# All of the second batch's keys transposed on TensorE and scored in float32

## The chip, the cores and the metric

The kernel runs on one core of a Trainium2 chip. The metric is the device time of one execution in microseconds (us); below it is compared by the median of several runs. The engines have short names in the profile: PE is TensorE (its weight loads are PEld), DVE is VectorE, ACT is ScalarE, POOL is GpSimd, SP is SyncE, which issues nearly all DMAs here.

## The reference

Two stages follow each other for 4 batches of 11456 tokens of width 128. First an attention through 49 agents: the agents attend to the keys and gather values, then the queries attend to the agents. Then a mixture of 8 experts of width 1024, of which each token takes one.

```python
def sm(a, b):
    s = scale * (a @ b.transpose(0, 2, 1))
    s = s - s.max(-1, keepdims=True)
    e = np.exp(s)
    return e / (e.sum(-1, keepdims=True) + 1e-09)
a2k = sm(agents, k)
agent_v = a2k @ v
q2a = sm(q, agents)
x = q2a @ agent_v
...
logits = xn @ en.T / tau
expert_idx = np.argmax(logits, axis=1)
...
h = np.maximum(x[mask] @ w1[e], 0.0)
out[mask] = gate_w[mask, None] * (h @ w2[e])
```

## The kernel before, in words

**Units.** The tokens of a batch are cut into `NU` = 12 units: 11 of 128 x 8 tokens and a last one of 96 x 2. A unit of keys, values or queries is one load of 512 KB by SP into one of `LB` = 10 buffers of a ring, which all three kinds share. `room()` lets a new load into the program's order when the unit that held the buffer has been marked by `used()` some steps earlier.

**Keys.** The scores of keys against agents need the keys with the width of 128 on the partitions, so each unit is transposed first. There are two ways to do it, and `by_pairs(b, u)` chooses for each unit of batches 1 to 3.

- `k1_f32`: PE transposes the 8 blocks of the unit as float32 into PSUM (`pe_T`, L420, tile `fTp`), ACT copies them to SBUF in two pieces (L427, tile `fT`), PE multiplies them with the agents in float32 (`scores`, L438; 16 matmuls of 64 columns of weights), ACT copies the scores out (L460), and DVE updates a running maximum (L410). The unit's buffer is marked as used as soon as the transposes are in the program.
- `k1_pairs`: ACT squares the unit to find a scale (L526), three small DVE instructions make a power of two of it (L251 to L255), ACT writes the scaled unit as float16 (L530), DVE writes the float16 remainder (L536), both into the tile `ks`, of which there are `XS` = 2. SP issues a DMA that transposes it in SBUF (L541, tile `kT`). PE multiplies with three float16 matmuls for each block (L550 to L552), ACT copies the scores out with a scale (L556), DVE updates the maximum (L410). The buffer is marked as used only after L536.

**The rest of a batch's preparation.** When all key units have a maximum, `k_max` reduces it; `k2_unit` takes exponentials and multiplies them with the values (L572, L577, L586); `av_chain` and `pick_expert` make one expert's weights ready for the batch in the form the main loop wants (tiles `gh`, `gl`, `w2p`, `vm`; loads of `w1s` and `w2s`, L907 and L908; rank and selection on DVE and ACT, L807, L809, L819, L895).

**The main loop.** A batch has 23 tiles of 512 tokens. A tile has two steps; each is a pair of matmuls (L1218, L1219, tile `hp`), an activation on ACT (L1222), a remainder on DVE (L1223), and 12 small matmuls into the output tile `yp` (L1246 to L1248). I call such a step an hp, and count the program's order of each engine in hp: 46 to a batch. Around it stand the queries (`q_unit`: transposes L420, scores L438, exponentials on ACT and a cast L955, remainder on POOL L956, a DMA transpose of `tt` by SP, L967), a proof that no token was treated wrongly (L1089 on PE, L1093 on ACT or L1095 on DVE), and the stores of the result (L1268).

**Order.** Batch b + 1 is prepared while batch b runs through the main loop. `plan()` gives each unit a due time in steps of the loop; `loader()` asks for loads 18 steps ahead of that if the ring has room. Batch 1's first `NEXT` = 4 key units are done before the main loop, all in float32. A scheduler then orders each engine's instructions when the kernel is built, and each engine runs its list strictly in that order. So a wait of one instruction holds up all that stand behind it on its engine.

`by_pairs` is the whole rule before:

```python
def by_pairs(b, u):
    return u % 2 == 0
...
spawn((k1_pairs if by_pairs(b, u) else k1_f32)(b, u))
```

Of the kernel before, what the change touches and what calls it, by code (L numbers as in the profile page):

```python
# [29 lines left out]
def kernel(ctx: ExitStack, tc: tile.TileContext, q, k, v, agents, emb, tau, w1, w2, out):  # L30
# [1559 lines left out]
        return sorted(kv), qs  # L1590

    def by_pairs(b, u):
        return u % 2 == 0

    AHEAD2 = 18

# [16 lines left out]
    def keys():  # L1613

        start = now[0] // 2
        for at, kind, b, u in plan()[0]:
            while now[0] // 2 < start + at:
                yield 1
            if kind == "k":
                if not hasattr(batches[b], "blks"):  # L1620
                    k_start(b)
                spawn((k1_pairs if by_pairs(b, u) else k1_f32)(b, u))
            else:
                kb = batches[b].blks[0]
                if u == 0:
                    while kb.k1 < NU:
                        yield 1
                    yield from k_max(b, pss, 1)
                    yield 1
                spawn(k2_unit(b, u, pool, (3, 4)))  # L1630
                if u == NU - 1:
                    spawn(after_keys(b))
# [31 lines left out]
    with nullcontext():  # L1664
        due = []
        for i in range(len(ticks) + LAG):
            if i < len(ticks):
                b, t, r = ticks[i]
# [12 lines left out]
            while due and due[0][0] <= i:  # L1681
                _, b, t, f = due.pop(0)
# [44 lines left out]
```

## Time and profile before

| | us |
|---|---|
| median of 3 runs | 694.39 |
| the runs | 689.1, 694.39, 697.4 |
| the profiled execution | 692.29 |
| its span, first to last instruction | 690.5 |

The profiled execution took 1.8 us more than its span, and lies 2.1 us below the median. The stages in it: batch 0's keys, values and weights up to about 87 us, then the main loops of the four batches, of which batch 0's lasts to about 245 us. Batch 1's and the first of batch 2's keys are worked on in this stretch. A row of the windows view has, for each engine, its busy time in the stretch and the number of instructions, then the granted clock of PE and the busy share of the DMA engines.

### The profile page before, as it was taken

What the parts mean: (1) busy time and instruction counts of PE and PEld (TensorE: products, weight loads), DVE (VectorE), ACT (ScalarE), POOL (GpSimd) and SP (SyncE); (2) the same over time, 40 slices, a digit from 0 to 9 for tenths busy, and PEclk for the clock granted to TensorE, in tenths of its full rate; (3) what the DMA queues carried; (4) which work ended last, traced back from release to release, by engine and by line L of the source; (5) the groups of instructions that cost most, each with busy time, mean ns of one, the idle gap of its engine ahead of it and who ended that gap; (6) DMA issues with size and microseconds to landing.
All of it is one profiled execution on the core that took longest, in us unless ns stands there. A gap on an engine that the chain in (4) does not pass through costs nothing. (4 is left out here: it accounts for less than half of the span.)

```text
span 690.5 us, 23309 instructions
## 1 busy us (share of the span) xinstructions
PE 644.2 (93%) x9168; PEld 529.4 (77%) x9168; DVE 535.2 (78%) x1492; ACT 488.8 (71%) x1350; POOL 322.0 (47%) x565
## 2 busy tenths in 40 slices
PE   8999898999898799999999889999999989998996
PEld 6887786877787588778888768787888768786785
DVE  4755996875577998856677999897567899878993
ACT  3455677887678946878778965778656973878941
POOL 6000146575402654666533452667473452977400
PEclk9998999999999999999999999999999999999999
DMA  8988279859478459986896529959576246134221
GB/s 337 298 270 299 70 151 251 232 145 265 112 255 227 102 159 248 229 206 140 244 310 197 138 84 224 219 133 249 149 217 212 83 120 156 43 83 139 77 81 71
DMA packets 163137, 124.74 MB, mean 181 GB/s; under 512 B 82874, under 2 KB 139280, under 8 KB 163026
## 3 DMA queue, kind: packets, MB, share of 16 engines
q1 hardware_dynamic: 162706, 123.01, 65.5%
q8 instruction: 73, 1.20, 0.7%
q14 instruction: 38, 0.31, 0.1%
q0 software_dynamic: 320, 0.23, 0.1%
HBM read 80.26 MB, written 23.79 MB: 151 GB/s over the span
## 5 line engine op out<-in xcount | busy, mean ns | idle before, releaser
L1223 DVE SCALAR_TENSOR_TENSOR hl<-hp,hh 128x512 f16<-128x512 f32 (+1 forms) x184 | 122.9, 669 | 30.2 <-ACT hh L1222 29.4
L1246 PE MATMUL yp<-w2p,hh 128*128 128x128 f16 x720 | 138.8, 221 | 1.8 <-ACT hh L1222 1.7
L1247 PE MATMUL yp<-w2p,hh 128*128 128x128 f16 x720 | 138.4, 221 | 0.0
L1093 ACT ACTIVATE under<-vp 128x320 f16<-128x320 f32 (+1 forms) x268 | 118.4, 442 | 26.9 <-PE vp L1089 24.2
L1248 PE MATMUL yp<-w2p,hl 128*128 128x128 f16 x720 | 136.2, 221 | 0.3 <-DVE hl L1223 0.3
L1222 ACT ACTIVATE hh<-hp 128x512 f16<-128x512 f32 (+1 forms) x184 | 107.6, 589 | 39.6 <-PE hp L1219 29.8
L1089 PE MATMUL vp<-vm,tt 128*128 128x320 f16 x360 | 96.1, 301 | 9.3 <-DVE vmin L1095 3.2
L438 PEld LDWEIGHTS sp<-aT_all,fT 128*64 128x64 f32 x2336 | 81.6, 140 | 20.7 <-issue 10.1
L438 PE MATMUL sp<-aT_all,fT 128*64 128x49 f32 x2336 | 94.7, 227 | 1.7 <-DVE rt L998 0.4
L427 ACT COPY fT<-fTp 128x512 f32<-128x512 f32 (+1 forms) x136 | 74.8, 573 | 27.6 <-PE fTp L420 19.7
L1246 PEld LDWEIGHTS <-hh 128*128 128x128 f16 x720 | 71.8, 100 | 18.4 <-ACT hh L1222 6.9
L1248 PEld LDWEIGHTS <-hl 128*128 128x128 f16 x720 | 71.7, 100 | 12.2 <-issue 2.9
L1247 PEld LDWEIGHTS <-hh 128*128 128x128 f16 x720 | 71.6, 99 | 5.2 <-issue 0.3
L1218 PE MATMUL hp<-tt,gh 128*128 128x512 f16 (+1 forms) x184 | 69.1, 376 | 4.1 <-ACT under L1093 2.1
L956 POOL TENSOR_TENSOR e<-qe,e 128x392 f16<-128x392 f32 (+1 forms) x46 | 40.2, 873 | 69.3 <-ACT e L955 66.5
L1040 POOL TENSOR_TENSOR nrm<-qq,half 128x16 f32<-128x16 f32 (+2 forms) x28 | 69.3, 2475 | 0.2
L1219 PE MATMUL hp<-tt,gl 128*128 128x512 f16 (+1 forms) x184 | 69.0, 376 | 0.0
L1261 DVE TENSOR_TENSOR ot<-yp,gs 128x512 f32<-128x512 f32 (+1 forms) x92 | 61.6, 671 | 7.2 <-PE yp L1248 4.3
L1237 PE MATMUL yp<-lin,tt 128*128 128x128 f16 x720 | 61.6, 220 | 2.2 <-DVE ot L1261 2.2
L1001 POOL TENSOR_TENSOR rt<-rt 128x384 f32<-128x384 f32 (+1 forms) x48 | 40.7, 848 | 45.5 <-DVE rt L998 43.2
L420 PE MATMUL fTp<-ident,qt 128*128 128x128 f32 (+1 forms) x344 | 53.3, 278 | 7.0 <-ACT under L1093 4.0
L1093 ACT ACTIVATION_READ_ACCUMULATOR under<-vp 128x1 f32 (+1 forms) x268 | 55.0, 205 | 0.0
(354 smaller groups left out, 1538.6 us busy)
## 6 DMA issues: line engine op xcount, KB each, us to landing
kt<-in_k_dram SPq DMA_DIRECT2D x44, 512.0 KB, 6.3
vt<-in_v_dram SPq DMA_DIRECT2D x44, 512.0 KB, 6.2
out_dram<-ot SPq DMA_DIRECT2D x88, 256.0 KB, 3.7
qt<-in_q_dram SPq DMA_DIRECT2D x42, 512.0 KB, 5.3
w1s<-in_moe_w_dram SPq DMA_DIRECT2D x9, 512.0 KB, 3.6
w2s<-in_moe_w_dram SPq DMA_DIRECT2D x9, 512.0 KB, 4.9
q<-in_q_dram SPq DMA_DIRECT2D x2, 512.0 KB, 11.9
tt<-e SPq DMA_TRANSPOSE x46, 3.3
```

The source lines that it names most:

```text
L427: act.copy(dst, tp[:, : m * p])
L438: i = pe.matmul(out=s[h : h + w, c * A : (c + 1) * A], lhsT=xT[:, c * p + h : c * p + h + w], rhs=rhs, start=True, stop=True, skip_group_c ...
L1040: pool.tensor_tensor(out=nrm, in0=quad, in1=half[:, :n], op=ALU.pow)
L1089: pe.matmul(out=z[:p, :FV], lhsT=tts[b, u][:, c * p : (c + 1) * p], rhs=bt.vm, start=True, stop=True)
L1093: act.activation(under[:p], z[:p, :FV], AF.Relu, scale=-1.0, accum_out=bt.vsum[:p, at])
L1218: pe.matmul(out=hp[:, :m], lhsT=bt.gh[:, fs], rhs=tt, start=True, stop=False)
L1219: pe.matmul(out=hp[:, :m], lhsT=bt.gl[:, fs], rhs=tt, start=False, stop=True)
L1222: h_last[:] = [act.activation(hh[:, :m], hp[:, :m], AF.Relu)]
L1223: dve.scalar_tensor_tensor(out=hl[:, :m], in0=hp[:, :m], scalar=0.0, in1=hh[:, :m], op0=ALU.max, op1=ALU.subtract)
L1246: pe.matmul(out=y, lhsT=hh[:, cs], rhs=wh, start=False, stop=False, skip_group_check=True)
L1247: pe.matmul(out=y, lhsT=hh[:, cs], rhs=wl, start=False, stop=False, skip_group_check=True)
L1248: y_last[:] = [pe.matmul(out=y, lhsT=hl[:, cs], rhs=wh, start=False, stop=last, skip_group_check=True)]
```

## The change

Batch 1 has no key unit by pairs any more; batches 2 and 3 keep every second one.

```diff
@@ -1590,7 +1590,7 @@
         return sorted(kv), qs
 
     def by_pairs(b, u):
-        return u % 2 == 0
+        return u % 2 == 0 and b > 1
 
     AHEAD2 = 18
```

Four units change their way, u = 4, 6, 8 and 10 of batch 1. Counted in the orders, PE gets 32 transposes (L420) and 64 float32 score matmuls (L438) more and 96 float16 matmuls (L550 to L552, 32 each) less; ACT gets 8 copies L427 and 4 copies L460 more, and 4 each of L526, L530 and L556 less; DVE loses 4 of L536 and 12 small ones; SP loses 4 DMA transposes L541. Everything after that is the scheduler's answer. The maximum of batch 1's keys (a transpose at L221 on PE) stands behind 13 hp in the order before and behind 10 in the changed one; batch 1's folded sums (L617) behind 30 and 28; its first selection matmuls (L828) behind 42 and 40; from batch 2's maximum on (56 and 57 hp) the two orders differ by at most two hp.

PE, batch 0's main loop around its sixth hp; before. `fTp<-ident,kt` is a key unit's transposes, `sp<-a_125,kT` the score matmuls of a pairs unit:

```order
L438 MATMUL sp<-aT_all,fT 64x49 x8
L1089 LDWEIGHTS tt
L1089 MATMUL vp<-vm,tt 128x320
L420 MATMUL fTp<-ident,kt 128x128 x8
L550 LDWEIGHTS kT
L550 MATMUL sp<-a_125,kT 128x49
L551 LDWEIGHTS kT
L551 MATMUL sp<-a_125,kT 128x49
L552 LDWEIGHTS kT
```

And the changed kernel's PE at its fifth hp:

```order
L438 MATMUL sp<-aT_all,fT 64x49 x16
L1089 LDWEIGHTS tt
L1089 MATMUL vp<-vm,tt 128x320
L438 MATMUL sp<-aT_all,fT 64x49 x16
L420 MATMUL fTp<-ident,kt 128x128 x8
L1248 LDWEIGHTS hl
L1248 MATMUL yp<-w2p,hl 128x128
```

The float16 scores are gone here, and key units in float32 follow each other closely: batch 1's last eight stand within the first ten hp, where they took twelve before.

ACT, batch 0's main loop at its eighth hp; before. `ks,ksq<-kt` is the Square of the fourth pairs unit of batch 1, `under` the proof, `hh` the main loop:

```order
L995 COPY rtg<-rtp 128x72
L1054 ACTIVATE ex<-lga 128x128
L526 ACTIVATE ks,ksq<-kt 128x8x128
L1093 ACTIVATE under,vsum<-vp 128x320
L1222 ACTIVATE hh<-hp 128x512
L995 COPY rtg<-rtp 128x72
```

And the changed kernel's ACT one hp earlier, behind the same kind of copy and exponential (`fT` is a copy of a float32 key unit's transposes, `qe` and `e` are a query's):

```order
L995 COPY rtg<-rtp 128x72
L1054 ACTIVATE ex<-lga 128x128
L427 COPY fT<-fTp 128x512 x2
L950 ACTIVATE qe<-qe 128x392
L955 CAST e_1_143<-qe 128x8x49
L1222 ACTIVATE hh<-hp 128x512
```

The Square that stood ahead of the proof and the main loop's activation has no successor; there are copies out of PSUM instead.

SP, batch 0's main loop around its 26th hp; before. `out_dram<-ot` are stores, `tt<-e` the query's DMA transpose, and the last `kt` is the load of the third pairs unit (u = 4) of batch 2:

```order
L157 DMA kt<-in_k_dram 128x1024
L1268 DMA out_dram<-ot 128x512
L157 DMA qt<-in_q_dram 128x1024
L157 DMA kt<-in_k_dram 128x1024
L157 DMA qt<-in_q_dram 96x256
L1268 DMA out_dram<-ot 128x512 x2
L967 DMA_TRANSPOSE tt<-e_1_143 128x8x128
L157 DMA kt<-in_k_dram 128x1024
L541 DMA_TRANSPOSE kT<-ks 128x16x128
```

And the changed kernel's SP at the corresponding load:

```order
L1268 DMA out_dram<-ot 128x512
L157 DMA qt<-in_q_dram 128x1024
L157 DMA kt<-in_k_dram 128x1024
L157 DMA qt<-in_q_dram 96x256
L1268 DMA out_dram<-ot 128x512
L967 DMA_TRANSPOSE tt<-e_1_143 128x8x128
L157 DMA kt<-in_k_dram 128x1024
L157 DMA qt<-in_q_dram 128x1024
```

Ten stores stand ahead of that load in place of twelve. It still follows the eighth `tt<-e`, but the cast L955 behind which that one stands moved from the 26th hp to the 23rd in ACT's order, while the Square that reads the load (L526) stayed at the 28th.

## Rows read from the trace of the kernel before

**Rows 1.** The page's part 1: busy us, share of the span, instructions.
```profile
PE 644.2 (93%) x9168; PEld 529.4 (77%) x9168; DVE 535.2 (78%) x1492; ACT 488.8 (71%) x1350; POOL 322.0 (47%) x565
```

**Rows 2.** Windows of batch 0's main loop: engines' busy us, granted clock, DMA share, GB/s.
```profile
95.00:110.00 15.00, 15.00 (x245) 13.01 (x244) 12.10 (x30) 12.46 (x30) 8.26 (x14) 1.00 1.08 220
...
115.50:118.70 3.20, 0.30 (x3) 0.30 (x4) 0.67 (x4) 1.92 (x5) 0.00 (x0) 1.00 1.12 263
118.70:123.00 4.30, 4.05 (x44) 3.13 (x43) 3.69 (x9) 3.21 (x9) 2.52 (x6) 0.64 1.00 239
123.00:130.00 7.00, 7.00 (x121) 5.65 (x118) 5.67 (x11) 5.75 (x18) 5.60 (x4) 0.98 1.10 277
```

**Rows 3.** Waits from 113 to 122 us: total us, times, longest.
```profile
ACT ks L526 <- DMA kT<-ks: 3.5, 1, 3.5
PE fTp L420 <- ACT under L1093: 3.3, 2, 3.1
```

**Rows 4.** Timeline at the same place: start, duration, instruction, idle time before it.
```profile
114.00 4.22 SPq L541 DMA_TRANSPOSE kT<-ks  x1
...
116.78 1.06 ACT L526 ACTIVATE ks<-kt 128x1024 f16<-128x1024 f32 x1 [3.45 <-DMA kT<-ks]
...
118.40 0.66 PE L420 MATMUL fTp<-ident,qt 128*128 128x128 f32 x4 [3.06 <-ACT under L1093]
```

**Rows 5.** Timeline from 14 us, float32 key units of batch 0 in a row.
```profile
14.82 1.01 PEld L438 LDWEIGHTS sp<-aT_all,fT 128*64 128x64 f32 x32 [0.17 <-issue]
...
15.89 0.86 PEld L420 LDWEIGHTS fTp<-ident,kt 128*128 128x128 f32 x8
...
16.91 1.01 PEld L438 LDWEIGHTS sp<-aT_all,fT 128*64 128x64 f32 x32 [0.17 <-issue]
```

**Rows 6.** Timeline, first and last of one pairs unit's 24 score matmuls.
```profile
109.72 0.19 PE L550 MATMUL sp<-a,kT 128*128 128x49 f16 x1
...
110.31 0.18 PE L552 MATMUL sp<-a,kT 128*128 128x49 f16 x1
```

**Rows 7.** Groups by line and shape: busy us, mean ns, idle before.
```profile
L427 ACT COPY fT<-fTp 128x512 f32<-128x512 f32 x128 | 72.2, 588 | 27.6 <-PE fTp L420 19.7 <-PE sp L438 6.3
...
L536 DVE SCALAR_TENSOR_TENSOR ks<-kt,hsc,ks 128x1024 f16<-128x1024 f32 x16 | 20.7, 1293 | 1.5 <-ACT ks L530 1.5
...
L530 ACT ACTIVATE ks<-kt,hsc 128x1024 f16<-128x1024 f32 x16 | 18.4, 1151 | 0.4 <-DVE hsc L253 0.4
...
L526 ACT ACTIVATE ks<-kt 128x1024 f16<-128x1024 f32 x16 | 17.0, 1062 | 6.8 <-DMA kT<-ks 3.5 <-DMA kt<-in_k_dram 3.4
...
L460 ACT COPY s_u<-sp 128x392 f32<-128x392 f32 x24 | 11.7, 486 | 19.7 <-PE sp L438 19.6
...
L556 ACT ACTIVATE s_u<-sp,hiv 128x392 f32<-128x392 f32 x16 | 9.5, 592 | 4.2 <-PE sp L552 4.2
...
L526 ACT ACTIVATION_READ_ACCUMULATOR ks<-kt 128x1 f32 x16 | 3.3, 204 | 0.0
```

**Rows 8.** Timeline around the third pairs unit of batch 2.
```profile
183.56 0.53 SPq L157 DMA_DIRECT2D kt<-in_k_dram  x1
...
188.34 1.06 ACT L526 ACTIVATE ks<-kt 128x1024 f16<-128x1024 f32 x1 [3.35 <-DMA kt<-in_k_dram]
...
189.96 0.38 PE L1218 MATMUL hp<-tt,gh 128*128 128x512 f16 x1 [1.82 <-ACT under L1093]
```

**Rows 9.** Window of batch 0's keys, all in float32.
```profile
15.00:25.00 10.00, 10.00 (x196) 8.84 (x194) 6.98 (x23) 4.42 (x9) 0.63 (x6) 1.00 1.08 338
```

**Rows 10.** Windows at the change from batch 0 to batch 1.
```profile
230.00:235.00 5.00, 1.94 (x17) 1.02 (x16) 4.88 (x14) 5.00 (x12) 4.11 (x11) 1.00 0.30 68
235.00:240.00 5.00, 4.54 (x37) 2.95 (x37) 4.89 (x19) 5.00 (x15) 2.25 (x6) 0.66 0.00 0
```

## The prediction

> **What bounds the kernel now.** I read the page's totals first. PE is busy 93% of the span, DVE 78%, ACT 71% [rows 1], so PE is the first suspect, but its ends are modelled, and a share over the whole span says little about a stretch. The change acts on 30 us or so of 690, so I went on to the windows of batch 0's main loop, where batch 1's keys are scored.
>
> From 95 to 110 us PE is busy without a gap, and its weight loads 13.01 of 15 us, or 87% [rows 2]. In the first stage, where PE does nothing but float32 key units one behind the other, the weight loads have 88% [rows 9]. So 87 to 88% is what PE shows when it issues all it can, and from 95 to 110 us PE is the bound. ACT with 12.46 and DVE with 12.10 of 15 us are not far behind.
>
> Then the picture breaks. From 115.5 to 118.7 us PE is busy 0.30 us of 3.2, and no other engine has much to do either [rows 2]. The waits of this place name two: ACT's Square of a pairs unit waits 3.5 us for the DMA that transposes an earlier unit's tile, and PE's transposes wait for ACT [rows 3]. The timeline has the order: SP needs 4.22 us for the issue of that DMA transpose, the Square starts at 116.78 us after 3.45 us of idle time, the proof behind it frees a PSUM bank, and PE goes on at 118.40 us after 3.06 us [rows 4]. There are only two tiles `ks`, so the fourth pairs unit must wait until an earlier one has been read by the DMA. I call this stall A. It has an aftermath: from 118.7 to 123 us the granted clock is 0.64, so PE spent part of the time at 1.2 instead of 2.4 GHz, after an idle stretch; from 123 us on it is 0.98 [rows 2].
>
> A second stall, B, lies at 185 to 190 us: the Square of batch 2's third pairs unit waits 3.35 us for a load that SP issued at 183.56 us, and PE waits 1.82 us behind it [rows 8].
>
> At the end of batch 0 the bound is another: from 230 to 240 us DVE is busy 9.77 and ACT 10.0 of 10 us, PE 6.48 [rows 10]. That is the choice of batch 1's expert, which the change moves by one or two hp but doesn't shorten.
>
> **The change part by part.** *PE gets more work.* A float32 unit costs 0.86 us for 8 transposes and 1.01 us for its score matmuls by the weight loads [rows 5], 1.87 us together; the period of such units was 2.09 us (14.82 to 16.91). The 24 float16 matmuls of a pairs unit run from 109.72 to 110.31 us, and with one more interval take 0.62 us [rows 6]. Each of four units so adds 1.25 us, in all 5.0 us. Since PE is the bound just where they go, I count all of it. The ends: 0, if it goes into PE's gaps, and 4 x (2.09 - 0.62) = 5.9 us, if each unit brings its small waits along.
>
> *Stall A goes.* The Square, and the DMA transpose that it waits for, are not in the program any more for batch 1; what stands at this place in ACT's order are copies out of PSUM, which wait for PE alone. That is worth 3.1 us [rows 4]. The clock comes back with it: PE was busy 4.05 us at 0.64 [rows 2], which is 4.05 x 0.64 = 2.6 us of work at full clock, so 1.5 us. The ends: 4.6 us, or nothing, if another wait takes its place (below).
>
> *Stall B.* Float32 units give their ring buffers back earlier, so batch 2's loads move up in SP's order. The load of stall B still follows the eighth query transpose, but that one's cast stands three hp earlier in ACT's order, while the Square that reads the load keeps its place. Three hp are more than the 3.35 us that were missing [rows 8]: batch 0's main loop, from about 87 to 245 us, took some 3.4 us for each of its 46 hp. I count the whole 1.8 us; the ends are 0 and 1.8. The unit ahead of it has the opposite case: its Square moves up by two hp, from the 24th to the 22nd, and so does its load. It waited for nothing before, so I count 0, with a bound of another 3.4 us, the length of stall B's wait.
>
> *ACT and DVE get less.* A pairs unit takes 1.06 + 0.20 + 1.15 + 0.59 = 3.0 us of ACT, a float32 unit 2 x 0.59 + 0.49 = 1.67 us [rows 7]; that frees 4 x 1.34 = 5.4 us of ACT. DVE loses 4 x 1.29 = 5.2 us [rows 7] and small instructions. Where PE is the bound this hides behind PE, so I count it at nothing; its cover is PE's unbroken work from 95 to 110 us [rows 2], and without that cover it would be a gain (below). SP gets rid of four issues like the one of 4.22 us [rows 4]; nobody but stall A waited for them in this stretch, so that is in the first term already.
>
> *The end of batch 0.* The first selection matmuls stand two hp earlier. DVE and ACT have the same work there as before, so I count 0.
>
> The sum, against the profiled execution's own 692.29 us: +5.0 - 3.1 - 1.5 - 1.8 = -1.4, so 690.9 us. The profiled execution was 2.1 us below the median of the runs; on the scale of the median the forecast is 694.4 - 1.4 = **693.0 us**. From the ends of the large terms: -6.4 (PE's work hidden, both stalls gone) to +5.9 (PE's work paid with its waits, nothing gained), which is 688.0 to 700.3 us.
>
> **A rule that speaks against this change.** In the first stage, where transposes are nearly half of PE's issue time, the granted clock is 1.00 from 15 to 25 us [rows 9]. The Trainium skill, "TensorE: Matmul & The Clock Gate", section "Part 4: PE-mode transpose", says that transposes don't count as activity of PE in the usual way, so that the full clock doesn't engage for them. By that rule, putting the float32 units closer together would let the clock fall where they stand; the trace speaks against it here, with 1.00 for five such units in a row.
>
> **The rivals.** *ACT sets the pace, and the gain is larger.* If PE's 5.0 us find room in gaps, and ACT's relief counts in full as well, the time falls by 6.4 to 6.4 + 5.4 = 11.8 us, to 682.6 to 688.0; I take 685. For it: ACT had 83% from 95 to 110 us, and all engines wait for each other in a strict order, so that relief at one can shorten a wait at another. Against it: PE's weight loads were at their full share in just that stretch [rows 2, 9].
>
> *Stall A comes back as waits for copies, and the kernel gets slower.* Eight float32 units follow each other within ten hp. Each needs two of the four PSUM banks that `hp` and the proof use as well, and two copies by ACT before PE may go on. In the first stage that cost only 0.17 us for each unit [rows 5], but ACT had 4.42 of 10 us to do there [rows 9], and DVE did half of the copies. In the main loop ACT does both and is busy 83%. If each unit waits for one more copy of 0.59 us [rows 7], that is 8 x 0.59 = 4.7 us, and with stall B left as it is the sum is 5.0 + 4.7 - 3.1 - 1.5 = +5.1, so 699.5 us; without the clock's and stall A's gain it is +9.7, so 704.1. It decides from the point at which the waits for ACT's copies before L420 and L438 exceed some 0.8 us for each of the eight units (what the forecast gains, 6.4 us, over eight). Against it: in the trace of before, key and query units stand beside each other too, and PE had no gap from 95 to 110 us.
>
> *The clock falls with the transposes.* If PE went at 1.2 GHz from 90 to 115 us, its 25 us of unbroken work there would take up to 25 us longer, some 718 us. Rows 9 speak against it.
>
> **How the numbers follow.** A measurement of this kernel can tell about 1% from no change: the three runs lie 8 us apart. 1% of 694.4 is 6.9 us, so faster means below 687.5 and slower above 701.3. Chances: the forecast with its ends 0.58 (all within 1%); the larger gain 0.20 (nearly all of it faster); waits for copies 0.20, of which half is above 701.3; the clock 0.02. So faster 0.20, within 1% 0.68, slower 0.12. The range leaves out the lower half of the larger gain and the upper half of the waits for copies: 685 to 701 us.
>
> **What would show it right or wrong.** In the changed kernel's profile there should be no wait of L526 for `kT<-ks` before 130 us, no stretch like 115.5 to 118.7 with PE idle, a granted clock near 1.00 there, and no wait of 1.8 us for a load near 185 us. PE's weight loads from 90 to 110 us should stay near 87%, and the tenth hp should come at about the time at which the twelfth or thirteenth came before. If L420 or L438 show waits for ACT's `fT` copies of over 5 us in all in batch 0's main loop, the slower rival holds. If PE's gaps there shrink and the end of batch 0 comes over 6 us earlier, ACT was the pace. The forecast is wrong as well if the shift by two hp changes what happens at the end of batch 0: PE lost 3.5 us there between 230 and 240 us [rows 10], and that can double or go.

## The result and the profile after

The changed kernel took 700.82 us in the median of 14 runs (697.94 to 704.27), the kernel before 697.38 us beside it. The ratio is 1.0068 with a 95% interval of [1.0049, 1.0086]: 4.7 us slower, between 3.4 and 6.0. The forecast was 1.4 us faster; the time lies inside its range, the sign is wrong. That it lies inside is luck: the upper end was there for stalls that stay and for waits for copies, and neither came. The ratios leave out runs over 1.5% above the fastest of their kernel, in experiment 17 two of twelve, and by the plain mean of all twelve its ratio would be 1.0023. The profiled execution took 704.27 us, the slowest of the 14, so its total doesn't stand against the 692.29 us of before; its stretches do, and experiment 12 is a second profile of the same kernel (698.73 us).

The page's part 1 of the changed kernel, as in [rows 1]:

```profile
PE 653.0 (93%) x9232; PEld 535.6 (76%) x9232; DVE 534.5 (76%) x1476; ACT 486.3 (69%) x1346; POOL 319.2 (45%) x565
```

PE has 64 instructions and 8.8 us more (the records hold each float32 score matmul twice, so 32 + 128 - 96), DVE and ACT have a little less. Then windows of the same kernel: four where [rows 2, 8] lay, three at the end of batch 0 as in [rows 10], and three longer stretches:

```profile
95.00:110.00 15.00, 15.00 (x260) 13.06 (x255) 9.82 (x24) 9.72 (x24) 6.80 (x16) 1.00 0.88 198
...
115.50:118.70 3.20, 3.20 (x70) 2.88 (x69) 2.86 (x7) 2.70 (x8) 2.54 (x6) 1.00 0.81 246
118.70:123.00 4.30, 4.30 (x88) 3.65 (x87) 2.85 (x6) 3.01 (x8) 3.87 (x7) 1.00 0.79 187
185.00:190.00 5.00, 5.00 (x74) 3.88 (x73) 3.14 (x7) 3.84 (x11) 1.87 (x3) 1.00 1.04 202
...
230.00:235.00 5.00, 1.37 (x6) 0.46 (x6) 4.96 (x13) 5.00 (x12) 0.49 (x2) 0.99 1.01 256
235.00:240.00 5.00, 4.18 (x27) 3.17 (x27) 4.01 (x16) 3.92 (x12) 1.50 (x2) 0.50 0.52 139
240.00:245.00 5.00, 5.00 (x45) 4.15 (x44) 3.17 (x13) 1.14 (x3) 0.76 (x5) 0.83 0.00 0
...
88.00:200.00 112.00, 112.00 (x1653) 90.89 (x1653) 78.26 (x178) 85.53 (x237) 58.74 (x93) 1.00 0.74 200
226.00:262.00 36.00, 29.57 (x369) 23.50 (x368) 29.04 (x83) 21.88 (x54) 13.81 (x31) 0.91 0.47 128
262.00:300.00 38.00, 32.97 (x538) 27.74 (x537) 31.36 (x97) 25.61 (x75) 20.33 (x41) 0.96 0.89 215
```

Both stalls are gone: PE is busy for all of 115.5 to 118.7 us and of 185 to 190 us, and the clock behind stall A is 1.00. At the end of batch 0 it has become worse. The last three windows of the kernel before, for the comparison:

```profile
88.00:200.00 112.00, 105.20 (x1578) 84.56 (x1577) 79.77 (x183) 87.25 (x237) 58.83 (x90) 0.98 0.82 205
226.00:262.00 36.00, 30.84 (x388) 24.72 (x388) 34.97 (x108) 25.73 (x70) 20.62 (x41) 0.95 0.47 129
262.00:300.00 38.00, 35.55 (x579) 29.12 (x576) 31.20 (x85) 27.95 (x85) 24.68 (x39) 1.00 0.98 245
```

I call a stretch's **loss** PE's idle time plus its busy time times what the clock lacks to 1.00. From 88 to 200 us the loss was 6.80 + 105.20 x 0.02 = 8.9 us and is 0. From 226 to 300 us it was 5.16 + 1.5 + 2.45 = 9.1 us and is 6.43 + 2.7 + 5.03 + 1.3 = 15.4 us. (Added up by windows of 2 us, as in the expectations below, it comes to about 9.4 and 15.9.) With PE's added 5.0 us, and 1.1 us more of idle time from 200 to 226 us, 5.0 - 8.9 + 6.3 + 1.1 = +3.5 us, inside the measured interval. The clock has two digits only, so each long stretch can be off by some half a microsecond. So the stalls' gain was made, and given back some 100 us later.

What PE waits for there is in the waits of the changed kernel from 226 to 300 us:

```profile
PE sqT L1303 <- DMA xq<-in_q_dram,ix: 4.5, 1, 4.5
POOL xq L1292 <- PE sqT L1303: 3.7, 1, 3.7
...
PE yp L1246 <- ACT hh L1222: 2.0, 1, 2.0
...
PE hp L1218 <- ACT under L1093: 1.4, 1, 1.4
```

The first of them is not among the waits of the kernel before. L1303 is the first step of the answer to batch 0's strayed tokens: POOL gathers their queries by an indirect DMA (L1293) with indices `ix` that DVE writes (L1167), and PE transposes them. Its timeline in the kernel before, rows of DVE, POOL and PE:

```profile
274.54 2.94 POOL L1040 TENSOR_TENSOR nrm<-qq,half 128x16 f32<-128x16 f32 x1
...
275.67 0.15 DVE L1167 SCALAR_TENSOR_TENSOR ix<-mine,none 128x1 int32<-128x1 f32 x1
...
278.72 1.29 POOL L1293 DMA_INDIRECT xq<-in_q_dram,ix  x1 [0.85 <-DVE ne L1199]
...
285.04 0.28 PE L1303 MATMUL sqT<-ident,xq 128*128 128x128 f32 x1
```

And in the changed one:

```profile
279.11 0.14 DVE L1167 SCALAR_TENSOR_TENSOR ix<-mine,none 128x1 int32<-128x1 f32 x1
...
279.58 3.14 POOL L1040 TENSOR_TENSOR nrm<-qq,half 128x16 f32<-128x16 f32 x1
282.93 1.29 POOL L1293 DMA_INDIRECT xq<-in_q_dram,ix  x1 [0.21 <-issue]
...
289.19 0.30 PE L1303 MATMUL sqT<-ident,xq 128*128 128x128 f32 x1 [4.49 <-DMA xq<-in_q_dram,ix]
```

In both kernels POOL issues the gather behind L1040, 3.1 us after the indices began to be written before and 3.8 us now. From its issue to its landing it took 4.2 us before and takes 6.1 us now. So it had landed at about 278.7 + 4.2 = 282.9 us, 2.1 us before PE came to L1303. Now it lands at 282.9 + 6.1 = 289.0 us, and PE is there at 289.19 - 4.49 = 284.70 us. The distance from the indices to PE's arrival fell from 9.4 to 5.6 us.

One would think that the order brought the two closer together. It didn't. The rows below count the hp ahead of `ix` in DVE's order (L1223 is DVE's instruction in each hp) and ahead of L1303 in PE's (L1218 opens an hp), each time before and then changed:

```profile
L1223 DVE SCALAR_TENSOR_TENSOR hl<-hp,hh x52: 350/682/692, 90.7 to 275.0; 128x512 f16<-128x512 f32 x50, 128x192 f16<-128x192 f32 x2
...
L1223 DVE SCALAR_TENSOR_TENSOR hl<-hp,hh x51: 305/681/693, 93.9 to 276.7; 128x512 f16<-128x512 f32 x49, 128x192 f16<-128x192 f32 x2
...
L1218 PE MATMUL hp<-tt,gh x54: 246/379/623, 87.0 to 282.9; 128*128 128x512 f16 x52, 128*128 128x192 f16 x2
...
L1218 PE MATMUL hp<-tt,gh x53: 244/379/583, 91.3 to 283.5; 128*128 128x512 f16 x51, 128*128 128x192 f16 x2
```

`ix` moved from behind the 52nd to behind the 51st hp and L1303 from behind the 54th to behind the 53rd: both by one, and two hp lie between them as before. What changed is when the engines come to them. DVE writes `ix` 5.0 us after PE has begun the hp ahead of it (274.11 us), where it was 2.5 us (273.16 us); PE comes to L1303 1.2 us after it has begun its last hp, where it was 2.1 us. The margin of 2.1 us, less 3.8 us of distance, 0.8 us on POOL and 1.9 us to the landing, makes -4.4 us, which is the wait. I call it **stall C**.

### The profile page after: what moved, and what is told of

Its sections match the earlier page's. It is cut to its first block, busy times and chain, and to the rows that moved or that the text cites. A ratio compares the mean times of both kernels' runs of the same rounds, so it can differ in the third digit from the quotient of the medians.

```text
span 702.5 us, 23405 instructions
## 1 busy us (share of the span) xinstructions
PE 653.0 (93%) x9232; PEld 535.6 (76%) x9232; DVE 534.5 (76%) x1476; ACT 486.3 (69%) x1346; POOL 319.2 (45%) x565
## 5 line engine op out<-in xcount | busy, mean ns | idle before, releaser
L1223 DVE SCALAR_TENSOR_TENSOR hl<-hp,hh 128x512 f16<-128x512 f32 (+1 forms) x184 | 122.8, 668 | 31.9 <-ACT hh L1222 30.7
L1222 ACT ACTIVATE hh<-hp 128x512 f16<-128x512 f32 (+1 forms) x184 | 107.7, 588 | 46.4 <-PE hp L1219 36.6
L438 PEld LDWEIGHTS sp<-aT_all,fT 128*64 128x64 f32 (+1 forms) x2464 | 87.0, 141 | 22.3 <-issue 11.8
L438 PE MATMUL sp<-aT_all,fT 128*64 128x49 f32 (+1 forms) x2464 | 100.9, 229 | 1.2 <-DVE aT_all L206 0.4
L427 ACT COPY fT<-fTp 128x512 f32<-128x512 f32 (+1 forms) x144 | 79.0, 574 | 24.0 <-PE fTp L420 18.3
L1218 PE MATMUL hp<-tt,gh 128*128 128x512 f16 (+1 forms) x184 | 69.5, 377 | 5.5 <-ACT under L1093 2.2
L1040 POOL TENSOR_TENSOR nrm<-qq,half 128x16 f32<-128x16 f32 (+2 forms) x28 | 68.5, 2445 | 0.0
L1237 PEld LDWEIGHTS <-tt 128*128 128x128 f16 x720 | 49.5, 100 | 10.8 <-issue 5.8
L420 PE MATMUL fTp<-ident,qt 128*128 128x128 f32 (+1 forms) x344 | 53.1, 276 | 3.6 <-ACT s_u L499 1.8
```

The source lines that it names most:

```text
L427: act.copy(dst, tp[:, : m * p])
L438: i = pe.matmul(out=s[h : h + w, c * A : (c + 1) * A], lhsT=xT[:, c * p + h : c * p + h + w], rhs=rhs, start=True, stop=True, skip_group_c ...
L1218: pe.matmul(out=hp[:, :m], lhsT=bt.gh[:, fs], rhs=tt, start=True, stop=False)
L1222: h_last[:] = [act.activation(hh[:, :m], hp[:, :m], AF.Relu)]
L1223: dve.scalar_tensor_tensor(out=hl[:, :m], in0=hp[:, :m], scalar=0.0, in1=hh[:, :m], op0=ALU.max, op1=ALU.subtract)
L1237: pe.matmul(out=yp[:p, c, :], lhsT=tc_, rhs=bt.lin[:, h], start=(c == 0 and h == 0), stop=False, skip_group_check=True)
```

## The experiments

All ratios are to the kernel before, on the same chip. The zero matmuls of some kernels are read by nobody, and no kernel leaves out work. The theories came one after the other; each ratio stands with its 95% interval. **T**: the loss comes from the selection two hp earlier. **P**: every float32 unit costs PE's time wherever it stands. **C**: the granted clock is lost because PE idles at the end of batch 0. **H**: what PE is late by is partly regained there. **D**: DVE and ACT are the bound there, with batch 2's pairs units among their work. **G**: stall C.

**1. The chain to the selection put back** to where it stood, by batch 1's share of the plan, in the changed kernel:

```diff
-        W_ = [(0, 0.19, 0.21, 0.45), (-0.66, 0.12, 0.16, 0.58), (-0.66, 0.12, 0.16, 0.58)]
+        W_ = [(0, 0.19, 0.26, 0.49), (-0.66, 0.12, 0.16, 0.58), (-0.66, 0.12, 0.16, 0.58)]
```

> All of batch 1's keys in float32 as in the changed kernel, but batch 1's values are due later (0.26 to 0.49 of batch 0's main loop in place of 0.21 to 0.45), so that in the orders batch 1's folded sums and selection stand behind the same hp as before the change (30, 42, 43 in place of 28, 40, 41). Theory T (the loss lies at the end of batch 0, where the selection of batch 1 comes two hp earlier): the loss goes, ratio to before 0.995 to 1.002. Theory P (PE pays for the float32 units, 1.25 us and its waits for each): the loss stays, ratio 1.005 to 1.009.

1.0056 [1.0021, 1.0091]. T fell. Its trace still has stall C, with 1.6 us, so this is no clean test of the rest. The loss from 226 to 300 us is 11.5 us there, some 4 us less than in the changed kernel, and the time is not clearly lower; but the trace is of the fastest of the 12 runs.

**2. Half of the change**, units 4 and 6 alone:

```diff
-        return u % 2 == 0 and b > 1
+        return u % 2 == 0 and (b > 1 or u > 6)
```

> Only units 4 and 6 of batch 1 change to float32; 8 and 10 stay pairs. Two pairs units find both ks tiles free, so stall A has no cause; the selection stands behind the same hp as before. Theory T: ratio 0.995 to 1.001, since stall A goes and the end of batch 0 is as before. Theory P: half of the loss, ratio 1.002 to 1.005.

1.0055 [1.0018, 1.0091]: slower, without stall C in its trace, and by the interval anything from a quarter of the whole change to more than all of it. T fell, and P's range ends just below, at 1.005. So a kernel can be this much slower without stall C, and this run speaks against stall C as the only cause.

**3. The kernel before, with an earlier selection:**

```diff
-        W_ = [(0, 0.19, 0.21, 0.45), (-0.66, 0.12, 0.16, 0.58), (-0.66, 0.12, 0.16, 0.58)]
+        W_ = [(0, 0.14, 0.16, 0.36), (-0.66, 0.12, 0.16, 0.58), (-0.66, 0.12, 0.16, 0.58)]
```

> Batch 1's keys as before the change (every second unit by pairs), but keys and values are due earlier (keys until 0.14, values 0.16 to 0.36 of batch 0's main loop), so that batch 1's folded sums stand behind 29 and its selection's first matmuls behind 39 hp in place of 30 and 42. Theory T: slower without a single float32 unit more, ratio 1.003 to 1.010. Theory P: no change from this, 0.997 to 1.003.

1.0163 [1.0115, 1.021], beyond both. Moving the plan by some hp is dear in itself, with a mean clock of 0.9705 (kernel before 0.984). It moves more than the selection, so it doesn't bring T back: its trace loses 12.6 us from 88 to 200 us and 10.0 us from 200 to 226 us, where the kernel before loses 8.9 and 1.9, and no more than the kernel before from 226 to 300 us.

**4. Batches 1 and 2 all in float32:**

```diff
-        return u % 2 == 0 and b > 1
+        return u % 2 == 0 and b > 2
```

> Batch 2's keys all in float32 too, ten units more than before in place of four. Selection of batch 1 behind 38 and 41 hp. Theory P: 0.17% for each unit, ratio 1.015 to 1.019. Theory T: six more units cost little; ratio 1.003 to 1.010, that is as the changed kernel.

1.0006 [0.9973, 1.0038]. Six more float32 units, and faster than the changed kernel: a price for each unit wherever it stands is refuted. T's range, from 1.003 up, was missed as well.

**5. The changed kernel, PE's idle time filled** with 16 zero matmuls, four behind each of the four rank steps (L807, L809) of batch 1's selection:

```diff
-            yield g
+            yield (b == 1 and zero_products(psx("fill"), 4, ())) or g
```

> The changed kernel with 16 matmuls of zeros by 512 columns more (3.4 us of PE at 0.215 us each), four behind each of the four rank steps of batch 1's selection; they stand at the 38th hp, where PE waits for ACT and DVE, and nothing reads them. Else the order is nearly that of the changed kernel. Theory C (the loss is lost clock: PE idles at the end of batch 0 behind the rank steps, and the granted clock falls there): the clock stays up, ratio to the kernel before 1.000 to 1.005, mean granted clock above the changed kernel's 0.980. Theory P (PE's own work in the first hp is the loss): no gain, or 3.4 us more, ratio 1.006 to 1.012.

1.0053 [1.0025, 1.008]. The mean clock rises from 0.980 to 0.987 and its loss from 226 to 262 us falls from 9.1 to 2.7 us, of which 3.4 us are the fill's own work; stall C stays with 4.3 us. The ratio is 0.15% below the changed kernel's, less than the uncertainty, so a gain isn't shown.

**6. The same fill in the kernel before** (same line).

> The kernel before with the same 16 matmuls of zeros, which stand here at the 39th and 40th hp. Theory C: a gain here too, since the kernel before loses clock at the same place (0.66 from 235 to 240 us), ratio 0.993 to 0.999. Theory P: no change, or up to 0.5% slower.

0.9983 [0.9956, 1.001]: inside C's range, but the interval holds 1, so neither a gain nor a price is shown.

**7. As much PE again** in the changed kernel, 6 zero matmuls (1.29 us) ahead of the scores of batch 1's units 4, 6, 8 and 10:

```diff
-        s = pss("sp")
+        s = pss("sp"); b == 1 and u % 2 == 0 and zero_products(s, 6, ())
```

> The changed kernel with six matmuls of zeros (1.29 us of PE) ahead of the scores of each of batch 1's units 4, 6, 8 and 10, so that the 5 us that the change adds to PE in the first nine hp are there twice; the order is else nearly that of the changed kernel. Theory P: another 0.5 to 0.75%, ratio 1.011 to 1.016. Theory C: PE catches up until the end of batch 0, where it waits for ACT and DVE anyway; ratio 1.004 to 1.009, as the changed kernel.

1.0174 [1.0143, 1.0205]: 1.06% above the changed kernel, 7.4 us for 5.2 us of PE (4.9 to 9.9 by both intervals). PE's time in the first nine hp is paid nearly in full or more, and C alone doesn't give this.

**8. Batch 2 alone in float32**, batch 1 as before:

```diff
-        return u % 2 == 0
+        return u % 2 == 0 and b != 2
```

> Batch 2's six pairs units in float32, batch 1's by pairs as before. The run with both batches in float32 had 1.0006. If the two changes add up, batch 2's alone is worth 0.6% gain: ratio 0.991 to 0.997 (theory C: batch 2's pairs units load ACT and DVE at the end of batch 0, where they are the bound). Theory P: six units cost 0.2 to 1%, ratio 1.002 to 1.010.

1.007 [1.0037, 1.0103]. Alone each batch costs 0.7%, both together nothing: the effects don't add, so what one of them costs hangs on the other.

**9. The PE time alone in the kernel before**, 5.2 us ahead of the scores of the four pairs units:

```diff
-        s = pss("sp")
+        s = pss("sp"); b == 1 and zero_products(s, 6, ())
```

> The kernel before with six zero matmuls (1.29 us of PE) ahead of the scores of each of batch 1's four pairs units, 5.2 us in all, read by nobody: as much PE as the change adds, but the pairs units with stalls A and B stay, and the selection at the end of batch 0 stays where it was. Theory P (PE's time in the first nine hp is paid in full, whatever else stands there): +5.2 us and no less clock, 1.006 to 1.010. Rival H (the end of batch 0 is bound by DVE and ACT, so that PE's delay ahead of it is partly regained there): 0.999 to 1.004.

1.0071 [1.0045, 1.0098], 4.9 us for 5.2. H fell: its range ends at 1.004. The interval, 3.1 to 6.8 us, leaves room for a smaller part that is regained.

**10. Half of the fill** in the changed kernel (2 in place of 4 in the line of experiment 5).

> The changed kernel with half of the earlier fill: two zero matmuls behind each of the four rank steps, 1.7 us in place of 3.4. Theory C (the changed kernel loses granted clock because PE idles at the end of batch 0; the fill gives the clock back, and its own time is paid): the clock as with the whole fill, 0.985 to 0.988, and 1.002 to 1.005. Rival (the gain of clock with the whole fill was that of other places and runs): clock 0.979 to 0.982 and 1.006 to 1.010.

1.012 [1.0078, 1.0161] with a mean clock of 0.981: C fell. The clock is the rival's, the time is above its range of 1.006 to 1.010, with an interval that reaches into it. The profile shows no loss of clock from 226 to 262 us, but stall C with 4.6 us, and clock lost at other places. Why it is slower than both no fill and the whole fill stays open.

**11. Experiment 4 with the whole fill.**

> Batches 1 and 2 both all in float32, with the whole fill (3.4 us). Without the fill this kernel was at 1.0006 with a mean clock of 0.9874. Theory C: there is hardly any clock left to win there, so the fill's time is paid, 1.003 to 1.007. Rival (the fill buys back about what it costs, as in the changed kernel): 0.998 to 1.001.

1.0037 [1.0004, 1.007]: inside C's range, where the fill only costs if no clock is lost; the interval reaches the rival's range and holds the 1.0006 of experiment 4, so the two aren't told apart.

**12. The changed kernel again.**

> The changed kernel itself once more, for a second profile of it and more times beside the kernel before. If the loss of clock at the end of batch 0 belongs to the kernel, the second profile has it at the same place, PE's idle time of 226 to 300 us again near 11 us with a granted clock below 0.9 in it, and the mean clock is 0.978 to 0.982; if it was one execution's, the place shows under 8 us of idle time and a clock above 0.95.

1.0083 [1.0049, 1.0116]. Its windows at the end of batch 0:

```profile
226.00:262.00 36.00, 29.70 (x405) 23.83 (x405) 32.60 (x101) 25.01 (x64) 14.03 (x33) 0.95 0.54 146
262.00:300.00 38.00, 32.88 (x499) 26.79 (x497) 29.82 (x85) 23.67 (x75) 21.41 (x38) 0.91 0.97 229
```

The loss is 6.30 + 1.5 + 5.12 + 3.0 = 15.9 us, against 15.4 in the first profile, and stall C is there with 4.6 us. The place belongs to the kernel and not to one execution.

**13 and 14. Late and early units of batch 2** in float32, in the kernel before; three units each:

```diff
-        return u % 2 == 0
+        return u % 2 == 0 and (b != 2 or u < 6)
```

> The kernel before, with only batch 2's units 6, 8 and 10 in float32: their pairs work on DVE and ACT (about 36, 42 and 48 hp) lies at the end of batch 0. Theory D (at the end of batch 0 DVE and ACT are the bound and PE idles, so that a pairs unit taken away there is a gain and its float32 work on PE lies in idle time): idle and lost clock from 226 to 300 us fall from 9.4 us to under 6, and 0.994 to 0.999. Theory P (PE's time is paid in full wherever it is put): 3 x 1.25 us more, 1.004 to 1.007.

```diff
-        return u % 2 == 0
+        return u % 2 == 0 and (b != 2 or u > 5)
```

> The counterpart: the kernel before with only batch 2's units 0, 2 and 4 in float32 (about 18, 26 and 30 hp), where PE is busy without a gap but for stall B. Theory D: 3.75 us of PE are paid, 1.8 us of stall B come back, and the end of batch 0 stays as before: 1.001 to 1.005. Theory P gives the same as for the late units, 1.004 to 1.007. If this one is as fast as the late units or faster, theory D falls.

The late units: 1.0022 [0.9985, 1.006]; the early ones: 1.0106 [1.0053, 1.016]. Windows of the kernel with the late units:

```profile
226.00:262.00 36.00, 33.70 (x477) 28.69 (x475) 33.70 (x102) 25.22 (x74) 17.73 (x41) 0.95 0.43 127
262.00:300.00 38.00, 37.57 (x557) 30.24 (x556) 29.85 (x87) 26.71 (x84) 22.93 (x38) 1.00 0.74 198
```

And of the one with the early units:

```profile
226.00:262.00 36.00, 29.37 (x339) 24.11 (x337) 33.79 (x106) 23.77 (x63) 18.65 (x40) 0.86 0.44 121
262.00:300.00 38.00, 36.66 (x616) 30.73 (x614) 33.27 (x98) 28.15 (x84) 23.05 (x40) 1.00 1.10 248
```

The loss is 2.30 + 1.7 + 0.43 = 4.4 us with the late units and 6.63 + 4.1 + 1.34 = 12.1 with the early ones. The three late units cost nothing that can be measured, the three early ones 7 us. D is right that the place matters and that the loss falls with the late units, but both of its times were missed: the gain of the late units (0.994 to 0.999) did not come, and the early ones cost more than 1.001 to 1.005. With the early ones the end of batch 0 didn't stay as before either (a loss of 12.1 us in place of 9.1, with a clock of 0.86), so the 7 us are not PE's work at its own place alone.

**15. The late units of batches 2 and 3** (`u % 2 == 0 and (b == 1 or u < 6)`).

> As with the late units of batch 2, and batch 3's units 6, 8 and 10 in float32 as well (82, 88 and 94 hp, at the end of batch 1, where PE idles 4.7 us and loses 1.7 us of clock from 380 to 420 us in the kernel before). Theory D: another 1 to 3 us gained, 0.990 to 0.997. Theory P: 6 x 1.25 us more, 1.009 to 1.012.

1.0131 [1.0079, 1.0184]. D doesn't carry over to the end of batch 1: there the idle time of 380 to 420 us stayed, 5.4 us. The time is P's, within its interval.

**16. The changed kernel with batch 2's late units** (`u % 2 == 0 and b > 1 and (b != 2 or u < 6)`).

> The changed kernel, with batch 2's units 6, 8 and 10 in float32 as well. Theory D: the 15.9 us of idle time and lost clock from 226 to 300 us fall below 9, and the time comes to 0.998 to 1.003. Theory P: 1.010 to 1.014.

1.004 [1.0006, 1.0075]. Three more float32 units, and the mean is 2.7 us below the changed kernel's (698.3 against 701.0 over 25 runs of other rounds). D's sign on the loss came, its time was missed by a little, P fell. Its loss from 226 to 300 us:

```profile
226.00:262.00 36.00, 33.03 (x449) 26.86 (x446) 31.02 (x95) 24.16 (x71) 13.62 (x33) 1.00 0.34 112
262.00:300.00 38.00, 37.27 (x606) 31.22 (x604) 31.50 (x90) 28.19 (x86) 25.02 (x44) 1.00 0.90 223
```

2.97 + 0.73 = 3.7 us, and no stall C in the waits. Here I saw what the kernels with all of batch 1 in float32 have in common: stall C is in the traces of experiments 1, 5, 7, 10 and 12, and in none in which batch 2's late units are in float32 too (4, 11, 16). In those three L1303 stands behind the 53rd hp as well; the gather lands sooner there, after 3.0 to 4.2 us, and PE comes 0.9 to 2.2 us after its landing.

**17. Stall C taken away.** In the changed kernel the answer starts later behind the gather, so that L1303 stands behind 57 hp in place of 53:

```diff
-        yield 22 if b < B - 1 else 14
+        yield (36 if b == 0 else 22) if b < B - 1 else 14
```

> The changed kernel, with the answer to batch 0's strayed tokens started later: 36 half steps behind the gather of their queries in place of 22, so that PE's transpose L1303 stands behind 57 hp (changed kernel 53, kernel before 54). Theory G: 4.5 us of what was given back at the end of batch 0 are PE's wait for that gather, which POOL issues at 282.9 us and which lands 6.1 us later, while in the kernel before PE came to it after it had landed; and the clock falls after that wait. Then no such wait is left, idle time from 262 to 300 us falls from 5.0 to under 1.5 us, and the time is 4 to 6.5 us below the changed kernel: 0.998 to 1.001. Rival D alone (ACT and DVE are the bound there, and the wait for the gather only stands where another would): 1.004 to 1.008, with the idle time of 262 to 300 us under other names.

0.9998 [0.9961, 1.0036]; the mean is 696.7 us against 701.0. Its windows:

```profile
226.00:262.00 36.00, 29.58 (x394) 23.63 (x391) 31.08 (x89) 23.42 (x58) 13.40 (x31) 0.91 0.49 131
262.00:300.00 38.00, 35.51 (x586) 29.40 (x582) 34.05 (x100) 28.20 (x87) 24.61 (x43) 1.00 1.06 251
```

From 226 to 262 us nothing changes (29.58 us of PE against 29.57). From 262 to 300 us PE's idle time falls from 5.03 to 2.49 us, not quite to the 1.5 expected, and the clock rises from 0.96 to 1.00; the gather is as slow as before (6.0 us to its landing), but PE doesn't come to L1303 before 293 us.

**18. The control**, the same later answer in the kernel before (same line).

> The control: the kernel before with the same later answer (36 half steps, L1303 behind 57 hp in place of 54). Theory G: PE came to L1303 after the gather had landed, so there is no wait to win: 0.998 to 1.002. Rival (a later answer is a gain for any kernel, and says nothing on the change): 0.992 to 0.996.

1.0053 [1.0011, 1.0095]. No gain; a small loss, above G's range of 0.998 to 1.002. So a later answer is no gain by itself, and what experiment 17 won belongs to the kernel with the wait. With the later answer in both kernels, 0.9998 against 1.0053, the change makes nothing slower.

The traces can be compared at the same step of the loop as well. The rows give the starts of the first and the 70th hp on ACT (L1222), in the kernel before, the changed kernel, its second profile (12), experiment 17 and experiment 18:

```profile
L1222 ACT ACTIVATE hh<-hp x70: 362/597/655, 88.5 to 339.0; 128x512 f16<-128x512 f32 x68, 128x192 f16<-128x192 f32 x2
...
L1222 ACT ACTIVATE hh<-hp x70: 348/597/647, 92.0 to 346.4; 128x512 f16<-128x512 f32 x68, 128x192 f16<-128x192 f32 x2
...
L1222 ACT ACTIVATE hh<-hp x70: 348/597/645, 88.1 to 341.9; 128x512 f16<-128x512 f32 x68, 128x192 f16<-128x192 f32 x2
...
L1222 ACT ACTIVATE hh<-hp x70: 350/597/644, 89.4 to 339.9; 128x512 f16<-128x512 f32 x68, 128x192 f16<-128x192 f32 x2
...
L1222 ACT ACTIVATE hh<-hp x70: 363/597/634, 88.4 to 339.3; 128x512 f16<-128x512 f32 x68, 128x192 f16<-128x192 f32 x2
```

That is 250.5, 254.4, 253.8, 250.5 and 250.9 us: to this step the change costs 3.3 to 3.9 us, and nothing once stall C is gone. The same rows to the 92nd hp, the end of batch 1:

```profile
L1222 ACT ACTIVATE hh<-hp x92: 331/597/655, 88.5 to 417.9; 128x512 f16<-128x512 f32 x88, 128x192 f16<-128x192 f32 x4
...
L1222 ACT ACTIVATE hh<-hp x92: 322/597/647, 92.0 to 423.4; 128x512 f16<-128x512 f32 x88, 128x192 f16<-128x192 f32 x4
...
L1222 ACT ACTIVATE hh<-hp x92: 323/597/645, 88.1 to 419.3; 128x512 f16<-128x512 f32 x88, 128x192 f16<-128x192 f32 x4
...
L1222 ACT ACTIVATE hh<-hp x92: 331/597/644, 89.4 to 420.8; 128x512 f16<-128x512 f32 x88, 128x192 f16<-128x192 f32 x4
...
L1222 ACT ACTIVATE hh<-hp x92: 330/597/634, 88.4 to 420.2; 128x512 f16<-128x512 f32 x88, 128x192 f16<-128x192 f32 x4
```

Here it is 329.4, 331.4, 331.2, 331.4 and 331.8 us. Between the two steps the kernel before takes 78.9 us, the changed one 77.0 and 77.4, and both kernels with the later answer 80.9, so in these single executions experiment 17 has no lead left. How its lower times over 12 runs come about behind this step isn't shown.

No version beats the kernel before by more than its uncertainty. Experiments 6 (0.9983), 17 (0.9998), 4 (1.0006) and 13 (1.0022) can't be told from it. Experiments 2, 3, 8, 9, 14, 15 and 18 are slower beyond their intervals without stall C; some of them add work for PE, but 3 and 18 add none. So a mere change of the order often costs something in this kernel, a rival that no run here rules out for a part of the loss.

## Why the forecast was wrong, point by point

**PE's added work, +5.0 us: right as far as the runs can tell.** It was counted in full, against the bounds 0 and 5.9. In the changed kernel itself it is inferred, from the sum that closes with it. Experiment 9 puts 5.2 us of PE at the same units of the kernel before, and it costs 0.71% or 4.9 us [3.1, 6.8].

**Stall A with its clock, -4.6 us, and stall B, -1.8 us: right.** The windows from 88 to 200 us have PE busy for all of 112 us at 1.00, where 8.9 us were lost. That is even 2.5 us more than counted: I had priced the two stalls that I had named, and the stretch had a few small ones more. The length of an hp that I used for stall B was too short, since batch 0's main loop doesn't end at about 245 us: its 46th hp starts at 257.2 us, the first at 88.5, which makes 3.7 us for each in place of 3.4. The step stands all the more.

**The signs.** The waits, the idle stretch, the clock and the load came as said, and the weight loads from 90 to 110 us are 16.76 of 20 us, 84%. One sign failed: the tenth hp should have come when the twelfth or thirteenth came before. It comes 36.6 us after the first, where the tenth came after 38.5 us before and the twelfth after 42.2. I give no cause for that.

**The rivals fell.** Of the first (ACT is the pace) the larger gain did not come: from 95 to 110 us ACT's busy time fell from 12.46 to 9.72 us and DVE's from 12.10 to 9.82, and PE was busy for all of it as before, its weight loads at 13.06 of 15 us. Of the second (waits for copies) the trace from 88 to 245 us has two waits of PE for `fT`, 1.2 us in total and both behind 200 us, where over 5 were its sign; neither is at L420 or L438. It named the right sign and nearly the right time, for a wrong reason. The third (the clock falls with transposes) is refuted with twice as many float32 units in that stretch: 1.00 from 88 to 200 us. The rule named for it, in the Trainium skill's "TensorE: Matmul & The Clock Gate", section "Part 4: PE-mode transpose", is again not what this trace shows, with 1.00 in a stretch where transposes stand between other matmuls; transposes alone were not run.

**The failed step is "The end of batch 0 ... so I count 0".** I reasoned that DVE and ACT have the same work there as before, and took the same work for the same time. Instructions that stand only a step or two elsewhere can meet at other times: the loss went from 9.1 to 15.4 us. The text itself said that the shift by two hp "can double or go" there. Of these 6.3 us, stall C and the clock behind it are the larger part. From 262 to 300 us experiment 17 brings the loss from 6.3 to 2.5 us, which was its size before the change. In the runs it is 0.70% (1.0068 to 0.9998, 4.9 us, with an interval of some 0.4% to either side), and then the kernel is at -0.1 us, 1.3 us from the forecast of -1.4. Up to the 70th hp the traces and the control agree that it is this wait; for the whole time it rests on the runs: experiment 17's interval ends below the changed kernel's, and its control gained nothing. The views shown ahead of the prediction end at 240 us; L1303 lies at 285 us, and no row of mine held the distance between the gather and its use.

**The rest, about 2.4 us from 226 to 262 us and 1.1 us just ahead of it** (idle time from 5.16 to 6.43 us, clock from 0.95 to 0.91), is shown as a place and not as a cause. Filling PE there restores the clock, and no gain in time can be told from the noise (experiment 5). Taking batch 2's late pairs units from DVE and ACT removes most of the loss (13, 16), which fits a bound by these two engines, but the same step failed at the end of batch 1 (15).

**That batches 1 and 2 together cost nothing** is explained in part: with batch 2's units in float32 too, stall C is not there. But batch 2's six units cost 0.7% alone (experiment 8), and that they cost nothing on top of a changed kernel without stall C stays open. **Open** as well are experiment 2, which is slower without stall C, experiments 3 and 10, 1.6 and 1.2% slower, and why a later answer costs something in experiment 18.

## What to carry to other kernels

When a change moves instructions by even one step of a loop, look for pairs of producer and consumer that lie on different engines (here a gather on one queue, its use on PE) along the whole distance for which the order is moved, and compare the distance of each pair in time, not in steps, with the producer's latency. Here producer and consumer moved by the same one step, and a margin of 2.1 us still became a wait of 4.5 us, because the indices came later within their step, the issue stood behind another instruction and the transfer took longer. Where two halves of a change don't add up, look for a wait that is there in one kernel and not in the other before pricing anything by the unit. And try extra work of an engine where that engine idles, but measure it at each place: three float32 units cost 0.2% at the end of batch 0 and 1.1% some 17 hp earlier, while another three at the end of batch 1 cost about 1.1% as well (1.0022 to 1.0131).

## What the runs showed of the hardware that was not expected

The indirect gather of the strayed queries took between 3.0 us (experiment 11) and 6.6 us (experiments 2 and 6) from its issue to its landing, in kernels that differ by a few units' loads and transposes around it.

POOL's L1040, a TENSOR_TENSOR of 128x16 that takes a power, lasted 2.94 and 3.14 us in the rows above, where other operations of that size beside it took 0.22 us (L1044, L1061). In the changed kernel the gather's issue stood behind it on POOL and began 0.2 us after its end.

The granted clock from 235 to 240 us was 0.50, which is 1.2 of 2.4 GHz, after 5 us in which PE was busy 1.37 us; from 240 to 245 us it was 0.83.
